# Chunked attention with a token-selecting feed-forward layer: V laid over 60 consecutive partitions, loaded on two queues

## The chip, the cores and the metric

One NeuronCore of a Trainium2 chip runs the whole program. The metric is device time in microseconds, from the first to the last instruction with what lies around them; lower is better. The program has five instruction streams (TensorE or PE, VectorE or DVE, ScalarE or ACT, GpSimd or POOL, SyncE or SP). DMAs are issued from SP and ACT (hardware queues) and from POOL (the software queue, the only one here whose DMAs cast from float32 to float16 on the way), and sixteen DMA engines carry them all out.

## The reference

Four batches, eight heads, 768 tokens of 64 numbers. The tokens are cut in chunks of 32. A chunk attends to eight memory keys and to the tokens from 16 before it to 8 after it:

```python
for c in range(nc):                      # 24 chunks of 32 tokens
    l_start, r_end = max(0, c_start - 16), min(S, c_end + 8)
    k_full = concat([mem_k, k[:, :, l_start:r_end]]); v_full = concat([mem_v, v[:, :, l_start:r_end]])
    scores = matmul(q_c, k_full.T) / sqrt(D)
    a = exp(scores - max); a = a / sum(a)
    out[:, :, c_start:c_end] = matmul(a, v_full)
# x = out with the heads side by side: (4, 768, 512); then per batch:
s = x @ w_gate; top = the 128 tokens with the largest s
ye = relu(x[top] @ w1) @ w2              # 512 -> 1024 -> 512
out[top] = x[top] + sigmoid(s[top]) * ye
```

## The kernel before

**Tiling.** Work goes by pairs of heads (head i and head i+4 of a batch): 16 pairs n = 0 to 15, four to a batch. Three chunks form a group of 96 queries, eight groups to a pair. The context of a group is 120 tokens in a row (16 before, 96, 8 after). Of them the 60 even-odd token pairs and four rows of memory make the 64 rows of one head; two heads fill the 128 partitions. A V row holds two tokens (128 float32, 512 B). `t[partition, pair and group, 128]` in `vbufs` holds one batch; there are two such buffers.

**The layout before.** Row 16 jj + t of a head's 64 partitions holds the token pair 4t + jj, and rows 15, 31, 47 and 63 hold memory. So one head's V takes four DMAs of 15 partitions (L96), and `mem_v` goes to four partitions, one DMA for each pair (L103). K is transposed on PE into `p_t` and copied by DVE into `kw` in the same order of columns (L225); POOL adds the memory columns (L232).

**Order.** `tc.manual_schedule()` keeps each engine's instructions in the order in which the code issues them, and an engine waits at the first of its instructions that isn't ready. The loop over n issues: scores of pair n+1 (PE matmuls L258, ACT exponentials L263), `tr_k` of n+2, values of n (PE, L284), `cast_v` of n+2 (ACT L240 for six groups, DVE L242 for the first and last), second half of the scores, `tr_q` of n+3, second half of the values, `normalise` (DVE L291, L292). The steps of the feed-forward layer of the batch before are spread over the four pairs of a batch by `moe_steps`. One of them is `m_x16` (L336): the cast of x to float16, in three DVE instructions for a batch.

**Loads.** The q and k of a batch go through POOL (L80, cast to float16), V through SP (a part of the first pair through ACT). Batch 0 is loaded at the start, batch 1 and the weights (`load_w`, L198, L199) after the prologue, batch b+2 after the third pair of batch b. A DMA gets one of eight completion semaphores for the hardware queues (another eight for the software queue), and waits until the earlier DMA with the same one has landed.

Of the kernel before, what the change touches and what calls it, by code (L numbers as in the profile page):

```python
# [26 lines left out]
def kernel(  # L27
# [13 lines left out]
    nc = tc.nc  # L41
# [40 lines left out]

    def load_v(b, p0, n, engines=(nc.sync, nc.sync)):


        t = vbufs[b % 2].rearrange("p n g d -> p (n g) d")
        for hh in range(2):
            eng = engines[hh]
            h = 4 * hh + p0
            lo = 1 if (b, h) == (0, 0) else 0  # L90
            hi = NG * n - 1 if (b, h + n) == (B - 1, H) else NG * n
            for jj in range(4):
                o = 64 * hh + 16 * jj
                base = (b * H + h) * HD + (2 * jj - 16) * D
                u = NG * p0
                eng.dma_start(out=t[o:o + 15, u + lo:u + hi, :],  # L96
                              in_=_dap(v, base + 96 * D * lo, [[8 * D, 15], [96 * D, hi - lo], [1, 128]]))
                if lo:
                    eng.dma_start(out=t[o + 2:o + 15, u, :], in_=_dap(v, base + 16 * D, [[8 * D, 13], [1, 128]]))
                if hi < NG * n:  # L100
                    eng.dma_start(out=t[o:o + 14, u + hi, :], in_=_dap(v, base + 96 * D * hi, [[8 * D, 14], [1, 128]]))
            for i in range(n):
                eng.dma_start(out=t[64 * hh + 15:64 * hh + 64:16, NG * (p0 + i):NG * (p0 + i + 1), :],  # L103
                              in_=_dap(mem_v, (b * H + h + i) * n_mem * D, [[2 * D, 4], [0, NG], [1, 128]]))


    alloc_batch(0)
    load_qk(0, q, q16s[0], 0, 2, 4)
    load_qk(0, k, k16s[0], 0, 2, 4)
    ident16 = cst.tile([128, 128], F16, tag="ident16")  # L110
# [6 lines left out]
    nc.gpsimd.dma_start(out=memk16, in_=_dap(mem_k, 0, [[D, n_mem], [n_mem * D, B * H], [1, D]]))  # L117
    for h0 in (1, 5):
        load_qk(0, q, q16s[0], h0, 3)
        load_qk(0, k, k16s[0], h0, 3)  # L120

# [4 lines left out]
    for pr, g in ((0, 0), (NP - 1, NG - 1)):  # L126
        nc.vector.memset(vbufs[0 if pr == 0 else 1][:, pr, g, :], 0.0)
    load_v(0, 0, 1, (nc.sync, nc.scalar))
    load_v(0, 1, 3)
    wgb = cst.tile([128, Dm], FP, tag="wgb")  # L130
    nc.sync.dma_start(out=wgb, in_=_dap(moe_w_gate, 0, [[0, 128], [1, Dm]]))

    pi = cst.tile([128, 1], I32, tag="pi")
    nc.vector.tensor_scalar(out=pi, in0=prow, scalar1=15, scalar2=None, op0=ALU.bitwise_and)
    pp = cst.tile([128, 1], FP, tag="pp")
    nc.vector.tensor_copy(out=pp, in_=pi)
    ismem = cst.tile([128, 1], FP, tag="ismem")
# [446 lines left out]
```

## Time and profile before

| | us |
|---|---|
| median of three runs | 194.24 (193.93 to 195.65) |
| the profiled execution, its own time | 193.39 |
| span from first to last instruction in it | 191.7 |
| PE busy | 116.6 (61%) |
| DVE busy | 89.0 (46%) |
| ACT busy | 72.4 (38%) |
| POOL busy | 31.1 (16%) |
| DMA share of the chain that ended last | 37% |

The profile is of one execution. Busy time is that of the whole span; the chain that ended last is followed back from the last instruction, at each step to what released it. GB/s count the bytes as they land, so a load that casts float32 to float16 counts half of what it reads.

### The profile page before, as it was taken

The numbers are of one execution on the slowest core, as the hardware profiler recorded it, in microseconds if no ns is written. First come the engines' busy times: TensorE is split into PE (matmuls) and PEld (weight loads), VectorE is DVE, ScalarE is ACT, GpSimd is POOL, SyncE is SP. The second block draws the span as 40 slices with busy tenths as digits, with TensorE's granted clock in tenths as the row PEclk, the third lists the DMA queues.
The fourth block names the chain that finished last, engine by engine and source line by source line (L and its number), as shares of the span: only waits on it lengthen the run. The fifth ranks groups of instructions, "written<-read, shape, count | busy, mean of one in ns | idle before, by whom it ended". The sixth has DMA issues, their size and how long they took to land.

```text
span 191.7 us, 5338 instructions
## 1 busy us (share of the span) xinstructions
PE 116.6 (61%) x2280; PEld 95.5 (50%) x2280; DVE 89.0 (46%) x285; ACT 72.4 (38%) x152; POOL 31.1 (16%) x55
## 2 busy tenths in 40 slices
PE   0052750799000006999998977799988676745840
PEld 0041640688000005878887656698657565423810
DVE  2222001451000014699943799942799693478010
ACT  0040801961000017776447588148595031110210
POOL 7400910106000000000230220001220000030030
PEclk9999999999999999999999999559995557885596
DMA  5999999999999697999999993900048200047304
GB/s 75 207 203 113 120 166 221 187 208 204 214 208 186 83 107 69 119 90 263 214 135 180 207 177 89 270 9 3 3 56 258 77 0 0 3 56 224 107 0 55
DMA packets 29681, 24.76 MB, mean 129 GB/s; under 512 B 1892, under 2 KB 25432, under 8 KB 29656
## 3 DMA queue, kind: packets, MB, share of 16 engines
q1 hardware_dynamic: 19976, 14.68, 43.4%
q0 software_dynamic: 9104, 9.47, 32.9%
q8 instruction: 18, 0.29, 0.7%
q10 hardware_dynamic: 576, 0.26, 0.6%
q14 instruction: 7, 0.06, 0.1%
HBM read 25.49 MB, written 7.34 MB: 171 GB/s over the span
## 4 chain that ended last, share of the span: by engine, by line
DMA 37%; DVE 25%; PE 22%; issue 6%; SPq 5%; ACT 1%; POOLq 1%; ACTq 0%; DVEq 0%
DMA v<-in_v_dram 25%; DMA v<-in_mem_v_dram 7%; DVE junk L329 6%; PE p_x L284 6%; DVE gr L366 5%; SPq L96 4%; PE p_m L428 4%; DMA out_dram<-x 3%; DVE x L292 3%; PE p_m L437 3%; PE p_t L208 3%; PE p_m L403 3%; DVE x L336 3%; DMA out_dram<-y,idx 3%; PE p_s L258 3%
## 5 line engine op out<-in xcount | busy, mean ns | idle before, releaser
L263 ACT ACTIVATE es<-p_s,maskb 128x256 f16<-128x256 f32 x96 | 38.5, 477 | 24.6 <-PE p_s L258 24.6
L284 PE MATMUL p_x<-vc,es 64*96 64x65 f16 (+1 forms) x768 | 32.0, 235 | 1.3 <-DVE x L292 0.7
L208 PE MATMUL p_t<-ident,k 96*64 96x96 f16 x256 | 11.9, 253 | 31.3 <-ACT qT L216 28.4
L284 PEld LDWEIGHTS <-es 64*96 64x96 f16 (+1 forms) x768 | 25.5, 136 | 6.2 <-issue 1.7
L242 DVE TENSOR_SCALAR vc<-v,ones 128x128 f16<-128x128 f32 x32 | 8.8, 343 | 39.8 <-DMA v<-in_v_dram 26.2
L240 ACT CAST vc<-v 128x768 f16<-128x768 f32 x16 | 13.5, 845 | 35.6 <-DMA v<-in_v_dram 26.9
L232 POOL COPY kw<-memkT 128x64 f16<-128x64 f16 x16 | 9.1, 566 | 104.1 <-DVE kw L225 67.3
L208 PEld LDWEIGHTS <-k 96*64 96x64 f16 x256 | 9.5, 141 | 32.9 <-issue 27.4
L258 PE MATMUL p_s<-qT,kw 64*64 64x96 f16 x512 | 23.4, 253 | 0.5 <-ACT es L263 0.5
L258 PEld LDWEIGHTS <-kw 64*64 64x64 f16 x512 | 18.3, 141 | 4.3 <-issue 2.0
L208 PE MATMUL p_t<-ident,q 96*64 96x96 f16 x256 | 12.5, 258 | 10.4 <-DVE kw L225 9.8
L225 DVE COPY kw<-p_t 128x512 f16<-128x512 f16 x32 | 12.1, 419 | 11.4 <-PE p_t L208 10.5
L208 PEld LDWEIGHTS <-q 96*64 96x64 f16 x256 | 10.3, 145 | 12.1 <-issue 10.6
L329 DVE SCALAR_TENSOR_TENSOR junk<-x,wgb 128x512 f32<-128x512 f32 (+2 forms) x30 | 16.0, 580 | 0.1
L292 DVE TENSOR_TENSOR x<-p_x,rd 128x768 f32<-128x768 f32 x16 | 15.3, 958 | 0.6
L216 ACT COPY qT<-p_t 128x768 f16<-128x768 f16 x16 | 13.0, 810 | 6.3 <-PE p_t L208 6.2
L441 POOL DMA_INDIRECT out_dram<-y,idx x4 | 6.8, 1701 | 49.8 <-DVE y L440 27.8
L366 DVE TENSOR_SCALAR gr<-brow,scr 128x768 f16<-128x768 f32 x24 | 13.3, 614 | 0.1
L291 DVE RECIPROCAL rd<-p_x 128x12 f32<-128x12 f32 x16 | 3.7, 229 | 18.6 <-PE p_x L284 18.6
L403 PEld LDWEIGHTS <-x 128*128 128x128 f16 x96 | 9.8, 143 | 1.3 <-DVE sel L395 0.7
L428 PEld LDWEIGHTS <-w_sb 128*128 128x128 f16 x128 | 8.8, 110 | 3.2 <-DVE gate L418 2.4
L376 PEld LDWEIGHTS <-gr 128*128 128x128 f16 x144 | 5.4, 105 | 8.2 <-DVE gr L366 7.8
(89 smaller groups left out, 112.0 us busy)
## 6 DMA issues: line engine op xcount, KB each, us to landing
v<-in_v_dram SPq DMA_DIRECT2D x20, 240.0 KB
out_dram<-x SPq DMA_DIRECT2D x4, 1152.0 KB
q<-in_q_dram POOLq DMA_DIRECT2D x6, 384.0 KB, 12.8
k<-in_k_dram POOLq DMA_DIRECT2D x6, 384.0 KB, 13.4
w_sb<-in_moe_w_dram POOLq DMA_DIRECT2D x2, 1024.0 KB, 22.3
out_dram<-x SPq DMA_DIRECT2D x4, 384.0 KB
v<-in_v_dram SPq DMA_DIRECT2D x8, 180.0 KB
v<-in_v_dram SPq DMA_DIRECT2D x4, 232.5 KB
```

Source lines behind the costliest of these rows:

```text
L208: nc.tensor.transpose(out=p_t[64 * h:64 * h + 64, j, 2:98], in_=src[b][:, pr + 4 * h, 64 * j:64 * j + 64], identity=ident16[0:96, 0:96])
L216: nc.scalar.copy(out=qT, in_=p_t[:, :, 2:98].rearrange("p j t -> p t j"))
L225: nc.vector.tensor_copy(out=kw[:, :, s, :].rearrange("p g (j t) -> p g j t", t=16), in_=_sap(p_t, 100 * s, [[12, NG], [200, 4], [1, 16]]))
L240: nc.scalar.copy(out=vc[:, 1:7, :, 0:64], in_=vt[:, pr, 1:7, :].rearrange("p g (s d) -> p g s d", d=D))
L258: nc.tensor.matmul(out=p_s[o:o + 64, s, 96 * gi:96 * gi + 96], lhsT=kw[o:o + 64, g, s, :], rhs=qf[o:o + 64, 96 * g:96 * g + 96], start=Tru ...
L263: nc.scalar.activation(out=es[:, :, :, 32 * c:32 * c + 32], in_=pv[:, :, :, 32 * c:32 * c + 32], func=AF.Exp, bias=maskb[:, c:c + 1], scal ...
L284: nc.tensor.matmul(out=p_x[r0:r1, h, c0:c0 + 65], lhsT=es[o:o + 64, s, gi, q0:q1], rhs=vc[o:o + 64, GROUPS[half][gi], s, :], start=(s == 0 ...
L292: nc.vector.tensor_tensor(out=xs[b].rearrange("p g (h n d) -> p n h g d", n=NP, d=D)[:, pr], in0=pv[:, :, :, 0:64], in1=rd.to_broadcast([1 ...
L329: nc.vector.scalar_tensor_tensor(out=o, in0=i, scalar=1.0, in1=w, op0=ALU.mult, op1=ALU.mult, accum_out=dst[:, bl:bl + 1])
L366: nc.vector.tensor_scalar(out=m.gr[:, bl, :], in0=m.brow, scalar1=m.scr[:, bl:bl + 1], scalar2=None, op0=ALU.is_lt)
L403: nc.tensor.matmul(out=p_e[:, 0, 128 * dch:128 * dch + 128], lhsT=m.x16[:, bl, 128 * dch:128 * dch + 128], rhs=m.sel[:, bl, :], start=(bl ...
L428: nc.tensor.matmul(out=p_h[:, 0, 128 * fi:128 * fi + 128], lhsT=w1_sb[:, dch, f0:f0 + 128], rhs=m.xeT[:, dch, :], start=(dch == 0), stop=( ...
```

## The change

V: a head's 60 token pairs go to 60 consecutive partitions in token order (o = 0 for the first head of a pair, 64 for the second), memory to the last four. The four 15-partition DMAs of a head become one of 60 partitions; the first head's goes on SP, the second's on ACT. All `mem_v` loads go on SP, behind the V loads. The columns of `kw`, the masks and `ones8` follow the same order. K is loaded ahead of q at the start, and batch 0 is loaded pair by pair. `m_x16` runs on ACT instead of DVE. Line numbers of the changed kernel are two to three higher from about L94 on (the cast of V is L243, the copy of K L228, `m_x16` L339).

```diff
-    def load_v(b, p0, n, engines=(nc.sync, nc.sync)):
+    def load_v(b, p0, n, engines=(nc.sync, nc.scalar)):
         t = vbufs[b % 2].rearrange("p n g d -> p (n g) d")
+        u = NG * p0
         for hh in range(2):
...
-            for jj in range(4):
-                o = 64 * hh + 16 * jj
-                base = (b * H + h) * HD + (2 * jj - 16) * D
-                u = NG * p0
-                eng.dma_start(out=t[o:o + 15, u + lo:u + hi, :],
-                              in_=_dap(v, base + 96 * D * lo, [[8 * D, 15], [96 * D, hi - lo], [1, 128]]))
...
+            o = 64 * hh
+            base = (b * H + h) * HD - 16 * D
+            engines[hh].dma_start(out=t[o:o + 60, u + lo:u + hi, :],
+                                  in_=_dap(v, base + 96 * D * lo, [[2 * D, 60], [96 * D, hi - lo], [1, 128]]))
...
+        for hh in range(2):
             for i in range(n):
-                eng.dma_start(out=t[64 * hh + 15:64 * hh + 64:16, NG * (p0 + i):NG * (p0 + i + 1), :],
-                              in_=_dap(mem_v, (b * H + h + i) * n_mem * D, [[2 * D, 4], [0, NG], [1, 128]]))
+                nc.sync.dma_start(out=t[64 * hh + 60:64 * hh + 64, u + NG * i:u + NG * (i + 1), :],
+                                  in_=_dap(mem_v, (b * H + 4 * hh + p0 + i) * n_mem * D,
+                                           [[2 * D, 4], [0, NG], [1, 128]]))
...
+    load_qk(0, k, k16s[0], 0, 2, 4)
     load_qk(0, q, q16s[0], 0, 2, 4)
-    load_qk(0, k, k16s[0], 0, 2, 4)
...
-    for h0 in (1, 5):
-        load_qk(0, q, q16s[0], h0, 3)
-        load_qk(0, k, k16s[0], h0, 3)
+    for pr in range(1, NP):
+        load_qk(0, k, k16s[0], pr, 2, 4)
+        load_qk(0, q, q16s[0], pr, 2, 4)
...
-    load_v(0, 0, 1, (nc.sync, nc.scalar))
-    load_v(0, 1, 3)
+    load_v(0, 0, 1)
+    load_v(0, 1, 1)
+    load_v(0, 2, 2)
...
         for s in range(2):
-            nc.vector.tensor_copy(out=kw[:, :, s, :].rearrange("p g (j t) -> p g j t", t=16),
-                                  in_=_sap(p_t, 100 * s, [[12, NG], [200, 4], [1, 16]]))
+            nc.vector.tensor_copy(out=kw[:, :, s, 0:60].rearrange("p g (t j) -> p g t j", j=4),
+                                  in_=_sap(p_t, 100 * s, [[12, NG], [1, 15], [200, 4]]))
...
-        nc.gpsimd.tensor_copy(out=kw.rearrange("p g s (j t) -> p g (s j) t", t=16)[:, :, :, 15],
-                              in_=memkT[:, n:n + 1, :, :].rearrange("p o s j -> p o (s j)").to_broadcast([128, NG, 8]))
+        nc.gpsimd.tensor_copy(out=kw[:, :, :, 60:64],
+                              in_=memkT[:, n, :, :].unsqueeze(1).to_broadcast([128, NG, 2, 4]))
...
-        nc.vector.tensor_copy(out=o, in_=i)
+        nc.scalar.copy(out=o, in_=i)
```

**SP, from the last load of batch 0 to the refill of its buffer.** `v_0` and `v_1` are the two V buffers (`v_1` takes batch 1). Before:

```order
L131 DMA wgb<-in_moe_w_gate_dram 128x512
L96 DMA v_1_85<-in_v_dram 15x32x128 x4
L103 DMA v_1_85<-in_mem_v_dram 4x8x128 x4
L96 DMA v_1_85<-in_v_dram 15x32x128 x4
L103 DMA v_1_85<-in_mem_v_dram 4x8x128 x4
L96 DMA v_0_84<-in_v_dram 15x32x128 x4
```

Now, from the top of the queue:

```order
L94 DMA v_0_84<-in_v_dram 60x16x128
L103 DMA v_0_84<-in_mem_v_dram 4x8x128 x4
L133 DMA wgb<-in_moe_w_gate_dram 128x512
L94 DMA v_1_85<-in_v_dram 60x32x128
L103 DMA v_1_85<-in_mem_v_dram 4x8x128 x8
L94 DMA v_0_84<-in_v_dram 60x32x128
```

Eight V DMAs of batch 1 have become one, and all eight memory loads follow it; the other half has left this queue.

**ACT, from the cast of pair 1 to that of pair 2**, as it stands now, with the semaphores waited for (DMAHW: a DMA of a hardware queue):

```order
L219 COPY qT<-p_t 128x768 [waits PE_49]
L243 CAST vc_150<-v_0_84 128x12x64 [waits DMAHW4_49,DMAHW7_49,DMAHW1_49,DMAHW0_49]
L94 DMA v_1_85<-in_v_dram 60x32x128 [waits DMAHW2_49]
L266 ACTIVATE es<-p_s,maskb 128x8x32 [waits PE_49]
L266 ACTIVATE es<-p_s,maskb 128x8x32 x2
L243 CAST vc_153<-v_0_84 128x12x64 [waits DMAHW6_49,DMAHW5_49,DMAHW3_49]
```

The second half of batch 1's V is issued here, behind the cast of pair 1; before, no DMA stood between these casts.

**POOL, from the memory columns of pairs 0 and 1 to batch 1's loads** (DMASW: a DMA of the software queue). Before:

```order
L80 DMA k_0_87<-in_k_dram 96x3x512
L232 COPY kw_158<-memkT 128x64 [waits DVE_49]
L232 COPY kw_161<-memkT 128x64 [waits DVE_49]
L80 DMA q_1_354<-in_q_dram 96x4x512
L80 DMA k_1_355<-in_k_dram 96x4x512 [waits DMASW0_49]
```

Now:

```order
L80 DMA q_0_86<-in_q_dram 96x2x512 [waits DMASW0_49]
L235 COPY kw_148<-memkT 128x16x4 [waits DVE_49]
L235 COPY kw_151<-memkT 128x16x4
L80 DMA q_1_344<-in_q_dram 96x4x512 [waits DMASW1_49]
L80 DMA k_1_345<-in_k_dram 96x4x512 [waits DMASW2_49]
```

The copy for pair 1 no longer waits for DVE, and batch 1's q and k stand right behind it.

## Rows read from the trace of the kernel before

**Rows 1.** The page: busy time by engine, and 40 slices of the span.

```profile
PE 116.6 (61%) x2280; PEld 95.5 (50%) x2280; DVE 89.0 (46%) x285; ACT 72.4 (38%) x152; POOL 31.1 (16%) x55
...
DMA  5999999999999697999999993900048200047304
```

**Rows 2.** Chain that ended last, 0 to 75: start, us, what.

```profile
32.34 22.39 DMA v<-in_v_dram
...
57.96 12.92 DMA v<-in_mem_v_dram
```

**Rows 3.** Timeline of ACT: start, us, engine, line, names, shapes, count [idle before].

```profile
32.90 0.83 ACT L240 CAST vc<-v 128x768 f16<-128x768 f32 x1 [8.71 <-DMA v<-in_mem_v_dram]
...
42.81 1.20 ACT L263 ACTIVATE es<-p_s,maskb 128x256 f16<-128x256 f32 x3 [0.73 <-PE p_s L258]
70.95 0.84 ACT L240 CAST vc<-v 128x768 f16<-128x768 f32 x1 [26.94 <-DMA v<-in_v_dram]
```

**Rows 4.** Timeline of SP's queue, the issues of batch 1's V.

```profile
25.01 12.06 SPq L96 DMA_DIRECT2D v<-in_v_dram  x4
...
57.96 4.30 SPq L103 DMA_DIRECT2D v<-in_mem_v_dram  x4
```

**Rows 5.** Timeline of POOL, pair 1's memory columns and batch 1's first load.

```profile
18.89 0.45 POOL L232 COPY kw<-memkT 128x64 f16<-128x64 f16 x1 [6.62 <-DVE kw L225]
19.06 0.72 POOL L80 DMA_DIRECT2D q<-in_q_dram  x1
```

**Rows 6.** Busy time by stretch; the last two columns are DMA share and GB/s landed.

```profile
0.00:5.00 5.00, 0.00 (x0) 0.00 (x0) 1.61 (x16) 0.00 (x0) 3.74 (x12) 1.00 0.54 81
...
15.00:20.00 5.00, 1.97 (x41) 1.67 (x43) 1.35 (x4) 0.24 (x1) 1.11 (x3) 1.00 1.19 108
...
33.00:47.00 14.00, 12.29 (x264) 10.57 (x263) 6.11 (x20) 9.28 (x20) 2.99 (x6) 1.00 1.17 200
47.00:61.00 14.00, 0.94 (x23) 0.78 (x18) 0.00 (x0) 0.00 (x0) 1.17 (x2) 1.00 1.17 210
61.00:71.00 10.00, 0.00 (x0) 0.00 (x0) 0.03 (x1) 0.05 (x1) 0.00 (x0) 1.00 0.81 100
```

**Rows 7.** DMA issues of the whole run: names, queue, count, KB each (1,024 B).

```profile
v<-in_v_dram SPq DMA_DIRECT2D x20, 240.0 KB
...
q<-in_q_dram POOLq DMA_DIRECT2D x6, 384.0 KB, 12.8
...
w_sb<-in_moe_w_dram POOLq DMA_DIRECT2D x2, 1024.0 KB, 22.3
...
v<-in_mem_v_dram SPq DMA_DIRECT2D x31, 16.0 KB
wgb<-in_moe_w_gate_dram SPq DMA_DIRECT2D x1, 256.0 KB
```

**Rows 8.** DMA traffic from 143.9 to 150.5 us, the store of batch 2's x.

```profile
DMA packets 801, 1.59 MB, mean 241 GB/s; under 512 B 32, under 2 KB 32, under 8 KB 800
```

**Rows 9.** Instruction groups by shape: count, busy us, mean ns of one, idle before.

```profile
L292 DVE TENSOR_TENSOR x<-p_x,rd 128x768 f32<-128x768 f32 x16 | 15.3, 958 | 0.6
...
L240 ACT CAST vc<-v 128x768 f16<-128x768 f32 x16 | 13.5, 845 | 35.6 <-DMA v<-in_v_dram 26.9 <-DMA v<-in_mem_v_dram 8.7
...
L225 DVE COPY kw<-p_t 128x512 f16<-128x512 f16 x32 | 12.1, 419 | 11.4 <-PE p_t L208 10.5 <-ACT es L263 0.9
...
L336 DVE CAST x<-x 128x1024 f16<-128x1024 f32 x9 | 5.9, 686 | 0.0
```

**Rows 10.** Chain that ended last, in batch 1's first pairs.

```profile
85.47 1.20 DVE x L336 x2
```

**Rows 11.** Busy time by stretch, columns PE, PEld, DVE, ACT, POOL, in pair 5.

```profile
85.00:91.00 6.00, 6.00 (x120) 4.76 (x116) 5.81 (x16) 4.26 (x11) 0.46 (x1) 1.00 0.83 219
```

**Rows 12.** Timeline of DVE, the last two casts of x and what follows the first.

```profile
158.50 1.35 DVE L336 CAST x<-x 128x2304 f16<-128x2304 f32 x1
159.77 0.15 DVE L416 TENSOR_SCALAR idx<-p_m 128x1 int32<-128x1 f32 x1
...
174.38 0.55 DVE L336 CAST x<-x 128x768 f16<-128x768 f32 x1
```

More of the change, by code (lines that the diff above doesn't have):

```diff
@@ L81, in load_qk @@
                             in_=_dap(src, (b * H + h0) * HD, [[512, 96], [step * HD, n], [1, 512]]))
-    def load_v(b, p0, n, engines=(nc.sync, nc.sync)):
+    def load_v(b, p0, n, engines=(nc.sync, nc.scalar)):
         t = vbufs[b % 2].rearrange("p n g d -> p (n g) d")
+        u = NG * p0
         for hh in range(2):
-            eng = engines[hh]
             h = 4 * hh + p0
@@ L91, in load_v @@
             hi = NG * n - 1 if (b, h + n) == (B - 1, H) else NG * n
-            for jj in range(4):
-                o = 64 * hh + 16 * jj
-                base = (b * H + h) * HD + (2 * jj - 16) * D
-                u = NG * p0
-                eng.dma_start(out=t[o:o + 15, u + lo:u + hi, :],
-                              in_=_dap(v, base + 96 * D * lo, [[8 * D, 15], [96 * D, hi - lo], [1, 128]]))
[L98 to L101, printed above, removed]
+            o = 64 * hh
+            base = (b * H + h) * HD - 16 * D
+            engines[hh].dma_start(out=t[o:o + 60, u + lo:u + hi, :],
+                                  in_=_dap(v, base + 96 * D * lo, [[2 * D, 60], [96 * D, hi - lo], [1, 128]]))
+            if lo:
+                engines[hh].dma_start(out=t[o + 8:o + 60, u, :], in_=_dap(v, base + 16 * D, [[2 * D, 52], [1, 128]]))
+            if hi < NG * n:
+                engines[hh].dma_start(out=t[o:o + 56, u + hi, :],
+                                      in_=_dap(v, base + 96 * D * hi, [[2 * D, 56], [1, 128]]))
+        for hh in range(2):
             for i in range(n):
-                eng.dma_start(out=t[64 * hh + 15:64 * hh + 64:16, NG * (p0 + i):NG * (p0 + i + 1), :],
-                              in_=_dap(mem_v, (b * H + h + i) * n_mem * D, [[2 * D, 4], [0, NG], [1, 128]]))
+                nc.sync.dma_start(out=t[64 * hh + 60:64 * hh + 64, u + NG * i:u + NG * (i + 1), :],
+                                  in_=_dap(mem_v, (b * H + 4 * hh + p0 + i) * n_mem * D,
+                                           [[2 * D, 4], [0, NG], [1, 128]]))
     alloc_batch(0)
+    load_qk(0, k, k16s[0], 0, 2, 4)
     load_qk(0, q, q16s[0], 0, 2, 4)
-    load_qk(0, k, k16s[0], 0, 2, 4)
     ident16 = cst.tile([128, 128], F16, tag="ident16")
@@ L133 @@
     pi = cst.tile([128, 1], I32, tag="pi")
-    nc.vector.tensor_scalar(out=pi, in0=prow, scalar1=15, scalar2=None, op0=ALU.bitwise_and)
-    pp = cst.tile([128, 1], FP, tag="pp")
-    nc.vector.tensor_copy(out=pp, in_=pi)
+    nc.vector.tensor_scalar(out=pi, in0=prow, scalar1=63, scalar2=None, op0=ALU.bitwise_and)
+    kp = cst.tile([128, 1], FP, tag="kp")
+    nc.vector.tensor_copy(out=kp, in_=pi)
     ismem = cst.tile([128, 1], FP, tag="ismem")
-    nc.vector.tensor_scalar(out=ismem, in0=pp, scalar1=14.5, scalar2=None, op0=ALU.is_gt)
+    nc.vector.tensor_scalar(out=ismem, in0=kp, scalar1=59.5, scalar2=None, op0=ALU.is_gt)
     maskb = cst.tile([128, 3], FP, tag="maskb")
@@ L141 @@
     for c in range(3):
-        nc.vector.tensor_scalar(out=maskb[:, c:c + 1], in0=pp, scalar1=4.0 * c - 0.5, scalar2=None, op0=ALU.is_gt)
-        nc.vector.tensor_scalar(out=tmpm[:, c:c + 1], in0=pp, scalar1=4.0 * c + 6.5, scalar2=None, op0=ALU.is_lt)
+        nc.vector.tensor_scalar(out=maskb[:, c:c + 1], in0=kp, scalar1=16.0 * c - 0.5, scalar2=None, op0=ALU.is_gt)
+        nc.vector.tensor_scalar(out=tmpm[:, c:c + 1], in0=kp, scalar1=16.0 * c + 27.5, scalar2=None, op0=ALU.is_lt)
     nc.vector.tensor_tensor(out=maskb, in0=maskb, in1=tmpm, op=ALU.mult)
@@ L150 @@
     nc.vector.memset(ones8, 1.0)
-    nc.vector.tensor_scalar(out=ones8[:, 0:1], in0=pp, scalar1=1.5, scalar2=None, op0=ALU.is_gt)
-    nc.vector.tensor_scalar(out=ones8[:, 7:8], in0=pp, scalar1=14.0, scalar2=None, op0=ALU.not_equal)
+    nc.vector.tensor_scalar(out=ones8[:, 0:1], in0=kp, scalar1=7.5, scalar2=None, op0=ALU.is_gt)
+    nc.vector.tensor_scalar(out=ones8[:, 7:8], in0=kp, scalar1=55.5, scalar2=None, op0=ALU.is_lt)
+    nc.vector.tensor_tensor(out=ones8[:, 7:8], in0=ones8[:, 7:8], in1=ismem, op=ALU.max)
     vcs, kws = [], []
```

## The prediction, made before the changed kernel ran

> **What bounds the kernel now.** I read the page first: no engine is busy for more than 61% of the span, while the row of the DMA engines shows nines from the second slice to the 26th and little behind that [rows 1]. So the first two thirds are a matter of loads. The chain of waits says which: from 32 to 71 us its long pieces are landings of V and of the memory rows of V [rows 2]. The timeline of ACT shows where the engines stand still for them. There are two stalls. The first, 8.7 us, ends at 32.9, when the memory rows for pair 1 are there. The second, 26.9 us, ends at 70.95, when batch 1's V is there for the cast of pair 4 [rows 3]. ACT had been through with everything else at 42.81 + 1.20 = 44.0. From 70.95 on the program runs without a long wait for a load, and 191.7 - 70.95 = 120.75 us of the span follow. The question is therefore when the cast of pair 4 can start.
>
> Why V is late: SP issues batch 1's V from 25.0 to 62.3 [rows 4], in turn with POOL's q, k and weights. While both queues work, 200 to 210 GB/s land. While V is alone it is 100 to 108 GB/s, though the engines count as busy [rows 6]; a store of x, whose DMAs span 96 and 32 partitions, reaches 241 GB/s [rows 8]. The V loads, 15 partitions at a time, are slow by themselves. POOL also loses time: it waited 6.6 us for DVE before pair 1's memory columns, and batch 1's first q stood behind them, until 19.06 [rows 5].
>
> **The change part by part.**
>
> *V over 60 partitions, two queues.* What has to land before pair 4's cast: V of two batches (2 x 8 x 240 KB = 3.93 MB), their memory rows (2 x 8 x 16 KB = 0.26), the gate row (0.26), q and k of batches 0 and 1 (2 x 4 x 384 KB = 3.15; batch 0 is as many bytes in other pieces), and, ahead of it or beside it, the weights (2.10) [rows 7]: 9.70 MB. Batch 2's q and k (1.57) may come before or behind; with them it is 11.27 MB. In the first 5 us, 81 GB/s x 5 = 0.41 MB land. The rest at 205 GB/s, between the two rows with both queues at work [rows 6], takes (9.70 - 0.41) / 0.205 = 45.3 us, or 53.0 with batch 2's part: the cast starts at 50.3 or 58.0. The premise is that the stretches at 100 GB/s vanish, because the 60-partition halves land as freely as the store. I take 55, in the upper half, because SP's queue now holds all memory rows behind its half of V, and pair 4 needs the fifth of the eight. Gain: 70.95 - 55 = 15.95 us.
>
> The Trainium skill, page "SBUF — State Buffer", section "Door 1: The DMA port swizzle", says that 16 partitions in a row reach four of sixteen ports, at 104 GB/s measured for 1 MiB, and 64 reach eight, at 196. The trace agrees for the first: 108 GB/s. No row shows the second. By the page V alone would double its rate, which supports the premise and leaves the sum as it is.
>
> *POOL's copies no longer wait for DVE; k ahead of q; batch 0 by pairs.* They bring batch 1's q forward by up to the 6.6 us [rows 5], which is part of the uninterrupted rate above, and make pairs 0 and 1 ready sooner. Both lie ahead of the cast of pair 4, so I add nothing for them. That cover is gone only if V comes as early as pair 4 asks (first rival).
>
> *ACT issues a half of V.* The issue stands behind the cast of pair 1, so batch 1's second half can't start before that. It is one instruction, and the exponentials behind it would wait for the same loads anyway: nothing.
>
> *The copy of K on DVE.* 512 elements took 419 ns, reading 16 in a row [rows 9]. Now 480 are read with a step of 200 elements. At worst an element costs what the float32 product from PSUM costs, 958 / 768 = 1.25 ns: 599 ns, 0.18 more; at best nothing changes. I take 0.18, as the read is no longer in a row. In batches 1 to 3 DVE sets the pace in two of four pairs (5.81 busy of 6.00 in one [rows 11]); there it counts: 2 copies x 2 pairs x 3 batches x 0.18 = +2.2 us. The ends are 0 and, with all 22 copies from pair 5 on, +4.0.
>
> The Trainium skill, page "VectorE: DVE Perf Modes", section "Mode 2×_1P — pack two bf16 into one 32-bit read", wants a step of one between 16-bit elements for two results a cycle, which speaks against this part of the change. The 419 ns bear it out for the old order; by the rule the new order loses the pairing, and the sum stays.
>
> *The cast of x, from DVE to ACT.* On DVE three casts a batch, of which two stand in the chain: 1.20 us [rows 10], for three batches -3.6. The last batch's large cast stood for 159.77 - 158.50 = 1.27 us ahead of the index that the feed-forward layer waits for [rows 12]: -1.3. Its small one (0.55 [rows 12]) is ahead of the last mask: -0.5, or nothing if something else is late there. On ACT a cast of 1,024 columns costs 845 / 768 x 1024 = 1.13 us by V's cast [rows 9]. Two of three fall in pair 5, where ACT was busy for 4.26 of 6.00 us [rows 11]: 6.5 us of work in 6.0, so +0.5 us for each of three batches, +1.5. The ends are 0 (it runs into the next pair's room) and 9 x 1.13 = +10, which would need ACT on the path throughout; 3 is a fair end. Sum of DVE and ACT: 2.2 - 3.6 - 1.3 - 0.5 + 1.5 = -1.7, from -5.4 to +3.
>
> *The rest* (masks, one more operation on DVE at the start, the shape of POOL's copy) lies in time in which these engines waited for loads: nothing.
>
> **Sum.** 193.39 (the profiled execution's own time) - 15.95 - 1.7 = 175.7. The median of the runs is 0.85 above the profiled execution, so 176.6; I say **176**. With the cast at 50.3 or 58.0 and the ends of the DVE and ACT terms it is 168 to 183.
>
> **Rivals.**
>
> *A. V is served first.* Two hardware queues against one software queue may take two turns in three. Then V, q and k of two batches would land ahead of the weights: 4.46 + 3.15 = 7.61 MB, at 5 + 7.2 / 0.205 = 40 us. Pair 4 asks at 44.0 - 8.7 = 35.3 at the earliest, so 40 decides. Gain 30.9 instead of 15.95: 162. For it: the second hardware queue. Against it: one queue of V was slow beside POOL's, 25 to 71 us for 2.1 MB [rows 3, 4].
>
> *B. V is no faster.* The limit could lie in the 512-byte rows and not in the partitions, and then 60 at a time and two queues change nothing; only POOL's 6.6 us come back. The cast starts at 64.4: 193.39 - 6.6 - 1.7 + 0.85 = 186. For it: packets and bytes are the same. Against it: beside POOL's wide loads the same engines land twice as much [rows 6]. The Trainium skill, page "DMA: Bandwidth & Descriptors", section "Rules for kernel authors", says of two transfers to disjoint partition halves that they serialise, and that spreading DMAs over issuing engines brings no bandwidth. By that rule the second queue is worth nothing; the trace does not contradict it, since no row has two full halves at once.
>
> *C. Slower: the 60-partition DMA runs on few of the sixteen engines.* All DMAs of V would then sit on, say, four. An engine's share of 210 GB/s is 13 GB/s, four give 52, and 4.46 MB take 85 us: the cast starts at 87, 16 us later than now, 193.39 + 16 - 1.7 + 0.85 = 209. It turns slower where the cast starts after 70.95 + 1.7 = 72.7, that is under 4.46 MB / 71 us = 63 GB/s for V, fewer than five engines. Against it: the 15-partition DMAs moved 108 GB/s [rows 6], over eight engines' share, and 60 is a multiple of 15.
>
> **Chances.** My forecast 0.65, A 0.13, B 0.15, C 0.07. The likeliest, 176, is the prediction. 160 to 188 holds A, the forecast with its ends and B; C and an even earlier or later V stay out, some 0.15. This kernel's measurement tells about 1% (2 us) from no change. Faster by over 1%: the forecast, A and 0.10 of B, 0.88. Within 1%: 0.04 of B, where the copy of K and ACT eat the 6.6 us, and 0.01 of C: 0.05. Slower: the rest, 0.07.
>
> **What would show it.** The cast of V ahead of pair 4 starts at 50 to 58 and is still the longest wait of ACT. No stretch before it lands less than 150 GB/s after the first 5 us. POOL issues batch 1's q by 13 us. The copy of K takes near 0.6 us, the cast of x about 1.13 on ACT; the time from pair 4's cast to the end is 118 to 121 us. A wait on ACT of more than 0.5 us a batch behind a cast of x, a cast of pair 4 before 45 or after 62, or a longer tail after it would each show a term wrong.

## The result, and the profile after

The changed kernel takes **177.9 us** (median of 4 runs, 176.82 to 179.89). The kernel before took 194.94 beside it on the same chip (193.93 to 196.33): the ratio is 0.910, interval 0.901 to 0.919. Some executions of a kernel take a few per cent longer than its others; the medians here are of all runs, the ratios leave those out. The forecast was 176. The profiled execution took 178.1 us, its span is 176.3; that of before was 193.39 with a span of 191.7, so the span became 15.4 us shorter. The forecast had 15.95 + 1.7 = 17.65.

The page of the changed kernel answers [rows 1]. Engines first, then the 40 slices; the last row is the mean GB/s.

```profile
PE 118.3 (67%) x2280; PEld 95.9 (54%) x2280; DVE 88.5 (50%) x275; ACT 82.8 (47%) x163; POOL 28.5 (16%) x57
...
DMA  5999999999999898999920465000159000059104
GB/s 127 215 223 205 229 216 226 231 227 218 209 194 269 217 116 156 290 264 181 189 60 5 63 200 161 6 0 4 13 128 279 10 0 4 0 77 294 51 0 59
```

The nines now end with the 20th slice, not the 26th, and the GB/s under them stay above 200 from the second slice to the eleventh. The same stretches as in [rows 6] (the last two columns are DMA share and GB/s):

```profile
0.00:5.00 5.00, 0.00 (x0) 0.00 (x0) 1.62 (x16) 0.00 (x0) 3.74 (x12) 1.00 0.60 132
...
15.00:20.00 5.00, 2.36 (x48) 1.95 (x47) 1.46 (x3) 2.08 (x2) 4.48 (x14) 1.00 1.14 214
...
33.00:47.00 14.00, 9.57 (x208) 8.15 (x207) 4.05 (x8) 4.22 (x10) 2.64 (x6) 1.00 1.16 221
47.00:61.00 14.00, 8.93 (x192) 7.63 (x193) 7.48 (x19) 9.18 (x20) 0.24 (x1) 1.00 1.08 231
```

15 to 20 us went from 108 to 214 GB/s: the stretches in which V was alone and slow are gone. From 55 to 61 us, when batch 2's V is nearly alone, 260 GB/s land. The timeline of ACT shows what that did to the stalls of [rows 3], and a new one:

```profile
37.43 1.21 ACT L266 ACTIVATE es<-p_s,maskb 128x256 f16<-128x256 f32 x3 [0.73 <-PE p_s L261]
49.39 0.83 ACT L243 CAST vc<-v 128x768 f16<-128x768 f32 x1 [10.75 <-DMA v<-in_mem_v_dram]
49.69 0.33 ACTq L94 DMA_DIRECT2D v<-in_v_dram  x1
...
79.37 0.33 ACTq L94 DMA_DIRECT2D v<-in_v_dram  x1
79.74 5.86 ACTq L99 DMA_DIRECT2D v<-in_v_dram  x1
85.64 1.20 ACT L266 ACTIVATE es<-p_s,maskb 128x256 f16<-128x256 f32 x3 [5.75 <-issue]
```

Read it in three steps. The stall ahead of pair 1 is gone. The cast of pair 4 starts at 49.39, not 70.95: **21.56 us earlier**, where 15.95 were forecast, after a wait of 10.75 and not 26.94. But from there to the end of the span it is 176.3 - 49.39 = 126.9 us, against 120.75 before: **6.2 us of the gain are given back**. The lower three rows show where. ACT issues two V DMAs of batch 3 in a row, and the second one, 56 rows of 512 B (28 KB), occupies ACT's queue for 5.86 us; the exponentials behind it wait 5.75 us for "issue", that is for nothing that the profile can name. On DVE, the division that closes a pair shows the cost:

```profile
76.64 0.23 DVE L294 RECIPROCAL rd<-p_x 128x12 f32<-128x12 f32 x1 [0.44 <-PE p_x L287]
91.13 0.23 DVE L294 RECIPROCAL rd<-p_x 128x12 f32<-128x12 f32 x1 [8.61 <-PE p_x L287]
```

This pair takes 14.49 us. Two groups of instructions answer [rows 9], the copy of K and the cast of x (mean ns of one behind the comma):

```profile
L228 DVE COPY kw<-p_t 128x480 f16<-128x480 f16 x32 | 19.5, 650 | 13.7 <-PE p_t L211 13.7
...
L339 ACT CAST x<-x 128x1024 f16<-128x1024 f32 x9 | 9.7, 1077 | 0.0
```

POOL did not do as forecast either. The row that answers [rows 5] (issue of batch 1's first q) stands at 15.65, where the forecast said by 13 (it was 19.06):

```profile
15.30 0.41 POOL L235 COPY kw<-memkT 128x64 f16<-128x64 f16 x2 [7.20 <-DVE memkT L172]
15.65 0.70 POOL L80 DMA_DIRECT2D q<-in_q_dram  x1
```

POOL no longer waits for the copy of K, but 7.20 us for the memory keys: PE waits for their DMA until 13.89, where it was 9.15 before.

### The profile page after: what moved, and what is told of

Same layout as the page of the kernel before. It is cut to its first block, busy times and chain, and to the rows that moved or that the text cites. A ratio compares the mean times of both kernels' runs of the same rounds, so it can differ in the third digit from the quotient of the medians.

```text
span 176.3 us, 5308 instructions
## 1 busy us (share of the span) xinstructions
PE 118.3 (67%) x2280; PEld 95.9 (54%) x2280; DVE 88.5 (50%) x275; ACT 82.8 (47%) x163; POOL 28.5 (16%) x57
## 4 chain that ended last, share of the span: by engine, by line
DMA 31%; PE 28%; DVE 18%; ACT 7%; issue 7%; ACTq 4%; POOLq 1%; SPq 0%; DVEq 0%
DMA v<-in_v_dram 19%; PE p_x L287 8%; DMA v<-in_mem_v_dram 6%; DVE gr L369 6%; PE p_t L211 5%; DVE junk L332 5%; PE p_m L440 4%; DMA out_dram<-x 4%; PE p_s L261 4%; PE p_m L431 3%; ACTq L99 3%; PE p_m L406 3%; ACT es L266 3%; DMA out_dram<-y,idx 3%; DVE x L295 2%
## 5 line engine op out<-in xcount | busy, mean ns | idle before, releaser
L266 ACT ACTIVATE es<-p_s,maskb 128x256 f16<-128x256 f32 x96 | 38.9, 489 | 26.1 <-PE p_s L261 20.4
L228 DVE COPY kw<-p_t 128x480 f16<-128x480 f16 x32 | 19.5, 650 | 13.7 <-PE p_t L211 13.7
L243 ACT CAST vc<-v 128x768 f16<-128x768 f32 x16 | 13.8, 861 | 10.8 <-DMA v<-in_mem_v_dram 10.8
L211 PEld LDWEIGHTS <-q 96*64 96x64 f16 x256 | 10.1, 149 | 5.3 <-issue 4.2
L245 DVE TENSOR_SCALAR vc<-v,ones 128x128 f16<-128x128 f32 x32 | 7.6, 290 | 10.4 <-DMA v<-in_mem_v_dram 10.0
L339 ACT CAST x<-x 128x1024 f16<-128x1024 f32 (+2 forms) x11 | 12.6, 1148 | 0.0
L431 PE MATMUL p_m<-xeT,w_sb 128*128 128x128 f16 x96 | 7.2, 236 | 5.5 <-ACT hT L433 4.5
```

Source lines behind the costliest of these rows:

```text
L211: nc.tensor.transpose(out=p_t[64 * h:64 * h + 64, j, 2:98], in_=src[b][:, pr + 4 * h, 64 * j:64 * j + 64], identity=ident16[0:96, 0:96])
L228: nc.vector.tensor_copy(out=kw[:, :, s, 0:60].rearrange("p g (t j) -> p g t j", j=4), in_=_sap(p_t, 100 * s, [[12, NG], [1, 15], [200, 4]]))
L243: nc.scalar.copy(out=vc[:, 1:7, :, 0:64], in_=vt[:, pr, 1:7, :].rearrange("p g (s d) -> p g s d", d=D))
L266: nc.scalar.activation(out=es[:, :, :, 32 * c:32 * c + 32], in_=pv[:, :, :, 32 * c:32 * c + 32], func=AF.Exp, bias=maskb[:, c:c + 1], scal ...
L339: nc.scalar.copy(out=o, in_=i)
L431: nc.tensor.matmul(out=p_h[:, 0, 128 * fi:128 * fi + 128], lhsT=w1_sb[:, dch, f0:f0 + 128], rhs=m.xeT[:, dch, :], start=(dch == 0), stop=( ...
```

## The experiments

All kernels ran beside the kernel before (194.7 to 194.9 us); ratios are to it.

| kernel | us | ratio, interval |
|---|---|---|
| the change | 177.9 | 0.910, 0.901 to 0.919 |
| one queue for V | 183.16 | 0.940, 0.931 to 0.948 |
| one queue, 15 partitions at a time | 204.62 | 1.051, 1.043 to 1.060 |
| before, with early q and k | 194.54 | 0.984, 0.974 to 0.994 |
| small DMA on SP | 172.96 | 0.888, 0.881 to 0.895 |
| small DMA first, on ACT | 173.16 | 0.880, 0.871 to 0.888 |
| cast of x on DVE | 181.13 | 0.931, 0.926 to 0.937 |
| copy of K done twice | 188.26 | 0.964, 0.955 to 0.974 |
| small on SP, K read in a row | 179.77 | 0.933, 0.920 to 0.945 |
| small and memory rows first | 175.68 | 0.910, 0.899 to 0.920 |
| small on SP, weights late | **169.67** | 0.877, 0.862 to 0.891 |
| the same, V earlier | 173.50 | 0.891, 0.884 to 0.898 |

### V loads alone

Only batch 2's V is loaded, six times in six forms, each waited for by one small copy on DVE; all else of the computation is left out.

```python
    rows = t[o + 16 * jj:o + 16 * jj + 15] if form == "15row" else t[o + jj:o + 60:4]
...
for form, engs in (("15row", (SP, SP)), ("15step", (SP, SP)), ("60", (SP, SP)), ("60", (SP, ACT)),
                   ("15row", (SP, ACT)), ("15step", (SP, ACT))):
```

> Only V loads of one batch (1.97 MB), six times one after the other with nothing beside them; the rest of the program is left out. Order: four DMAs of 15 neighbouring partitions per half on SP; four DMAs of 15 partitions in steps of four per half on SP; one of 60 per half on SP; one of 60 per half, SP and ACT; then the first two forms with the halves on SP and ACT. If the reach of partitions is the limit (theory P): about 19 us (105 GB/s) for the first, 8 to 11 us (180 to 240 GB/s) for the second and third, 7 to 10 us for the fourth, and the fifth between 10 and 19 us. If the number of queues is what counts (theory Q): the first three alike, and the last three alike and faster. If the number of DMAs counts: the second as slow as the first, the third fast.

It ran once. The timeline of DVE; what stands in brackets is the wait for 1.97 MB of V:

```profile
25.46 0.19 DVE L72 COPY col<-vt 128x32 f32<-128x32 f32 x1 [20.34 <-DMA vt<-in_v_dram]
39.54 0.19 DVE L72 COPY col<-vt 128x32 f32<-128x32 f32 x1 [13.88 <-DMA vt<-in_v_dram]
52.25 0.20 DVE L72 COPY col<-vt 128x32 f32<-128x32 f32 x1 [12.52 <-DMA vt<-in_v_dram]
63.30 0.19 DVE L72 COPY col<-vt 128x32 f32<-128x32 f32 x1 [10.85 <-DMA vt<-in_v_dram]
81.06 0.19 DVE L72 COPY col<-vt 128x32 f32<-128x32 f32 x1 [17.56 <-DMA vt<-in_v_dram]
93.06 0.19 DVE L72 COPY col<-vt 128x32 f32<-128x32 f32 x1 [11.82 <-DMA vt<-in_v_dram]
```

On SP alone: four DMAs of 15 neighbouring partitions a half take 20.34 us (97 GB/s), four of 15 partitions with a step of 4 take 13.88, one of 60 takes 12.52 (157 GB/s). The second and the first have the same number of DMAs, rows and bytes; only the reach over partitions differs, and it makes 6.5 of the 7.8 us. A second queue takes 12.52 to 10.85, 13% less time, and the 15 neighbouring partitions from 20.34 to 17.56. The order is that of theory P; the second to fourth forms are slower than it had them (8 to 11 and 7 to 10 us).

The mean GB/s in 40 slices, first of the load with 60 partitions on one queue (39.9 to 52.2), then on two (52.6 to 63.2):

```profile
GB/s 0 0 30 147 230 301 226 203 223 191 148 143 143 160 186 160 158 170 190 188 182 190 223 206 203 206 196 195 195 190 195 195 195 186 193 163 75 7 0 0
```

```profile
GB/s 0 0 0 56 189 234 294 274 187 180 168 147 147 182 269 294 288 292 288 294 288 292 288 294 288 292 288 284 294 228 170 151 155 158 120 50 0 0 0 0
```

With two queues some 290 GB/s land through fourteen slices in a row; with one queue it is 143 to 230 in all slices but one between the first and the last few.

The Trainium skill, page "SBUF — State Buffer", section "Can I just issue two DMAs to hit both halves?", says that two DMAs at once, one at partition 0 and one at 64, gained 6% over a single one and that they serialise. Here the second queue gives 12.52 / 10.85 = 1.15 times the rate over the whole wait, and some 290 GB/s while both halves are under way, which the halves one after the other do not hold; the measurement decides, though over the whole wait the direction (much less than twice) agrees.

### One queue for V

```diff
-    def load_v(b, p0, n, engines=(nc.sync, nc.scalar)):
+    def load_v(b, p0, n, engines=(nc.sync, nc.sync)):
```

> The changed kernel with both halves of V on SP. Theory P: V still lands freely, so the cast of pair 4 starts at 50 to 56 us (49.4 with two queues), and as ACT then issues no DMA its stop of 5.9 us at 79.7 goes away; time 172 to 180. Theory Q: with one turn in two beside POOL's loads V is back where it was, the cast starts at 62 to 68, time 184 to 190.

183.16 us, 5.3 more than the change, although ACT now issues no V; with the 4.9 us that its hold costs the change (below) the second queue is worth up to 10.2. The time lies between the two expectations, and so does the cast of pair 4 at 59.84, some 10 us later than with two queues. The profiled execution is one of the two longest (189.0), so this row is a rough place only.

```profile
59.84 0.83 ACT L243 CAST vc<-v 128x768 f16<-128x768 f32 x1 [19.46 <-DMA v<-in_mem_v_dram]
```

So the second queue is worth more beside POOL's loads (some 10 us at the cast, for two batches of V) than alone (1.67 us for one batch). The Trainium skill, page "DMA: Bandwidth & Descriptors", section "Queues, rings and completion order", says that each DMA engine goes round between the queues that have work for it. By that, V with two of three queues gets more turns than with one of two; the two runs agree, but no run here separates this from a lesser hold on SP's own queue.

### One queue, 15 partitions at a time

The same with each half in four pieces, rows still in token order:

```diff
+            for jj in range(4):
+                engines[hh].dma_start(out=t[o + 15 * jj:o + 15 * jj + 15, u + lo:u + hi, :], ...
```

> As e1, both halves on SP and the same layout, but each half in four DMAs of 15 neighbouring partitions. Theory P: the stretches at about 100 GB/s come back and the cast of pair 4 starts 6 us or more later than in e1, 58 to 68; time 6 to 14 us over e1. Theory Q or POOL's earlier loads as the cause: within 3 us of e1.

204.62, so 21.5 us over the kernel with 60 at a time and more than before. Time and cast are both beyond either expectation. The stretches show the old sign again, 105 GB/s at a DMA share of 0.61 and 1.19:

```profile
70.73 0.83 ACT L245 CAST vc<-v 128x768 f16<-128x768 f32 x1 [19.51 <-DMA v<-in_v_dram]
...
61.00:71.00 10.00, 0.00 (x0) 0.00 (x0) 0.23 (x2) 0.27 (x1) 0.00 (x0) 1.00 0.61 105
71.00:85.00 14.00, 11.60 (x229) 9.69 (x229) 9.89 (x28) 10.63 (x23) 0.91 (x2) 1.00 1.19 105
...
90.48 0.61 PE L213 MATMUL p_t<-ident,k 96*64 96x96 f16 x10 [4.49 <-issue]
123.20 1.13 PE L289 MATMUL p_x<-vc,es 64*96 64x65 f16 x23 [4.99 <-issue]
```

At 70.73 the cast of pair 4 is back where it was before the change (70.95). So without the reach and the second queue, all other parts of the change together do not move this cast. The reach brings it to 59.84 and the second queue to 49.39: 10.9 and 10.5 us, about equal, as far as the one long execution with one queue goes.

The 21.5 us of the whole time are more than these 10.9. Behind the cast PE stands still for 4.49, 1.45 and 4.99 us, in the middle of a group of matmuls and for nothing that the profile names; with one queue and 60 partitions it is 2.01 and 2.98, and the kernel before has no such stop of 1 us. What causes them is not shown, so the whole time does not say what the reach is worth.

### Before, with q and k early

```diff
+    alloc_batch(1)
+    for h0 in (0, 4):
+        load_qk(1, q, q16s[1], h0, 4)
+        load_qk(1, k, k16s[1], h0, 4)
     mem_keys()
```

> The kernel before, with nothing changed but that batch 1's q and k are issued ahead of everything that POOL waits for in the prologue (in the changed kernel POOL has no such wait of 6.6 us). Theory of the prediction, rival B: this part alone brings batch 1's q forward by 6.6 us and at most that much comes off, 188 to 191. Rival: V's own 15-partition DMAs set the end and nothing comes back, 193 to 196; the first memory rows may even land later (V shares the engines with q earlier), up to 198.

The median is 194.54 (10 runs, 189.94 to 197.52), beside 194.86 for the kernel before. The ratio of 0.984 rests on the two shortest of the ten alone; by the medians no gain can be told from none. The profile says why: batch 1's q is issued at 7.00, 12 us earlier, and the stall is only moved.

```profile
43.54 0.83 ACT L240 CAST vc<-v 128x768 f16<-128x768 f32 x1 [19.48 <-DMA v<-in_mem_v_dram]
...
69.90 0.83 ACT L240 CAST vc<-v 128x768 f16<-128x768 f32 x1 [15.24 <-DMA v<-in_mem_v_dram]
```

Pair 1's wait grew from 8.71 to 19.48 us and pair 4's cast starts at 69.90, not 70.95. POOL's order alone brings 1 us at the cast of pair 4, and new waits for memory rows stand ahead of pairs 8 and 12 (4.15 and 1.10 us).

### The hold on ACT: small DMA on SP, and small DMA first

```diff
-                engines[hh].dma_start(out=t[o:o + 56, u + hi, :],
+                nc.sync.dma_start(out=t[o:o + 56, u + hi, :],
```

> The changed kernel with the one small DMA of the last group of batch 3 (56 partitions, 28 KB) issued on SP instead of ACT behind the large one. If ACT stands still there because a second DMA on its queue can't be issued until the large one ahead has been taken up (theory H): the stop of 5.9 us and the slower pair behind it (1.9 us) go, time 169 to 172.5. If other work would have been late there anyway: less than 2 us gained.

172.96 us. ACT issues one DMA in 0.33 us and goes on; SP's queue is occupied instead, where nothing waits (first ACT, then SP; how much of SP's 11.74 us is the same hold is not shown):

```profile
80.70 0.33 ACTq L94 DMA_DIRECT2D v<-in_v_dram  x1
81.37 1.20 ACT L266 ACTIVATE es<-p_s,maskb 128x256 f16<-128x256 f32 x3
```

```profile
69.93 11.74 SPq L99 DMA_DIRECT2D v<-in_v_dram  x1
```

The second form leaves both on ACT and only changes places: the issue of the 56 rows (then L95) stands ahead of the large one (L97).

> The changed kernel, in which the one place where ACT issues two DMAs of V in a row (batch 3, a small one of 28 KB behind one of 930 KB) has them in the other order, small one first, both still on ACT. Theory: an issue is held while a large DMA ahead of it on the same queue is being taken up; then the large one behind the small one is not held, ACT goes on within 1 us, and the time is that of the kernel that has the small one on SP (172.96), 172.5 to 174. Rival: two DMAs in a row on ACT hold it whatever their order (a queue that holds one): the hold of some 5 us stays, 177 to 179.

173.16 us, and no hold:

```profile
78.48 0.34 ACTq L95 DMA_DIRECT2D v<-in_v_dram  x1
78.91 0.35 ACTq L97 DMA_DIRECT2D v<-in_v_dram  x1
79.31 1.20 ACT L266 ACTIVATE es<-p_s,maskb 128x256 f16<-128x256 f32 x3 [0.25 <-ACT xeT L410]
```

So it is not two issues in a row that hold, but an issue behind a large one (31 x 60 rows of 512 B) on the same queue. The kernel with the cast of x on DVE, which has the order of the change, shows the hold again (4.96 us). By the medians the change pays 4.7 to 4.9 us for the order of two lines.

### Cast of x on DVE

```diff
-        nc.scalar.copy(out=o, in_=i)
+        nc.vector.tensor_copy(out=o, in_=i)
```

> The changed kernel with the cast of x back on DVE (m_x16, eleven instructions). Theory of the prediction: the change won 3.6 + 1.3 + 0.5 on DVE and paid 1.5 on ACT with this part, so putting it back costs 3.9 us: 177.9 + 3.9 = 181.8, the last pair of heads 2.0 to 2.6 us longer (10.55 us between its divisions before, 7.93 with the cast on ACT). Rival: DVE waits elsewhere in the middle batches and only the last batch counts (1.3 + 0.5 = 1.8, and 1.5 comes back on ACT): 178 to 180. A gain below 177 would say that ACT is the engine that the change overloads.

181.13: 3.2 us over the change, near the 3.9 of the prediction, and over the 178 to 180 of the rival. But the place is not the prediction's. The division of pair 2, first in the change, then here:

```profile
49.83 0.22 DVE L294 RECIPROCAL rd<-p_x 128x12 f32<-128x12 f32 x1
```

```profile
50.58 0.23 DVE L294 RECIPROCAL rd<-p_x 128x12 f32<-128x12 f32 x1
```

The last pair, from its predecessor's division to its own: in the change, here, and with the small DMA on SP (the third number from the right is the granted clock):

```profile
142.25:150.18 7.93, 6.25 (x110) 5.61 (x109) 4.28 (x18) 3.79 (x4) 0.00 (x0) 0.82 0.01 2
```

```profile
142.24:152.79 10.55, 7.55 (x110) 6.79 (x109) 5.55 (x19) 1.78 (x3) 0.00 (x0) 0.73 0.01 2
```

```profile
136.50:145.63 9.13, 7.45 (x110) 6.64 (x109) 4.29 (x17) 3.79 (x4) 0.00 (x0) 0.69 0.01 2
```

All casts of the first three batches lie between the divisions of pairs 2 and 14. That stretch takes 142.25 - 49.83 = 92.4 us in the change and 142.24 - 50.58 = 91.7 here: with the cast on DVE it is no longer. The last pair takes 10.55 and not 7.93, 2.6 us more. With the small DMA on SP and the cast on ACT it takes 9.13 at a clock of 0.69, so up to 1.2 of the 2.6 us may be the clock's and not the cast's (1 stands for 2.4 GHz, 0.5 for 1.2; these are means of both levels).

### Copy of K done twice

```diff
+            for _ in range(2):
                 nc.vector.tensor_copy(out=kw[:, :, s, 0:60]. ...
```

> The changed kernel with each copy of K out of PSUM done twice, 32 more copies of 0.65 us on DVE; 22 of them lie behind the cast of pair 4 in the program's order. Theory of the prediction: a microsecond of the copy counts in two of four pairs, 12 of 22 copies: +12 x 0.65 = 7.8 us, 185.7; by that slope the 0.23 us that a copy has grown cost 2.8 us. Rival 1: DVE has room, +2 us or less. Rival 2: each copy is on the path, since PE's transposes of q wait for the PSUM buffer that the copy empties: 22 x 0.65 = 14 us, 192.

188.26, 10.4 us more:

```profile
L229 DVE COPY kw<-p_t 128x480 f16<-128x480 f16 x64 | 40.5, 654 | 15.9 <-PE p_t L211 14.7
```

DVE works 40.5 - 19.5 = 21.0 us more, so a microsecond of the copy costs 0.50 us, between the prediction's way of counting (7.8) and rival 2 (14).

### K read in a row

```diff
-            nc.vector.tensor_copy(out=kw[:, :, s, 0:60].rearrange("p g (t j) -> p g t j", j=4),
-                                  in_=_sap(p_t, 100 * s, [[12, NG], [1, 15], [200, 4]]))
+            nc.vector.tensor_copy(out=kw[:, :, s, 0:60].rearrange("p g (t j) -> p g j t", j=4),
+                                  in_=_sap(p_t, 100 * s, [[12, NG], [200, 4], [1, 15]]))
```

> The changed kernel with the small DMA of batch 3's V on SP (172.96), and the copy of K walked in the other order: PSUM is read 15 elements in a row and kw written with a step of 4 elements, where the change reads with a step of 200 and writes in a row. Theory of the prediction (the step of the read costs the 0.23 us that a copy has grown): the copy falls to about 0.42 us, and by the slope of the doubled copies (10.4 us for 32 more of 0.65 us, 0.5 us for 1) 32 x 0.23 x 0.5 = 3.7 us come off: 169 to 170. Rival: a step on either side costs the same, the copy stays at 0.6 to 0.65 us and the time at 172 to 174.

179.77, 6.8 us over its base of 172.96, outside both expectations:

```profile
L228 DVE COPY kw<-p_t 128x480 f16<-128x480 f16 x32 | 38.7, 1313 | 14.3 <-PE p_t L211 14.3
```

The step that moved from the read to the write costs twice as much: 1,313 ns for 480 elements against 650. The change's choice, to read with a step and write in a row, is the cheaper of the two; 419 ns had both in rows. Here 38.7 - 19.5 = 19.2 us of DVE cost 6.8, 0.35 us for one (8.7 and 0.45 by the ratios, which take out the difference between chips). I first had the faster copy in mind and was wrong.

### Small ones first, memory rows too

```diff
+        if b > 0:
+            mem_rows()          # the eight mem_v DMAs of the batch, ahead of V
         for hh in range(2):
```

> The changed kernel with small ones first: the 28 KB DMA of batch 3 ahead of the large one on ACT (173.16), and for batches 1 to 3 the eight memory-row DMAs ahead of SP's half of V, not behind it. Theory: the cast of pair 4 waits for memory rows that SP could not issue while its large V DMA was being taken up; with them first, it waits for V alone, which has landed by 41 on SP and 46 on ACT (the same queues' landings in the run with the small DMA on SP): cast at 46 to 47.5 and 170.5 to 172. Rival: bytes set it, the memory rows land with the last of them anyway, and the cast stays at 48.5 to 51, 172.5 to 174.

175.68, 2.5 us over the kernel with the small DMA first alone. Pair 4 now waits for V, and longer:

```profile
53.65 0.83 ACT L248 CAST vc<-v 128x768 f16<-128x768 f32 x1 [15.41 <-DMA v<-in_v_dram]
```

SP's queue tells why: the eight memory DMAs take 9 us, and V is issued at 27.75, where it was 17.68 (first this kernel, then the one with the small DMA first alone).

```profile
17.64 9.03 SPq L91 DMA_DIRECT2D v<-in_mem_v_dram  x8
27.75 0.32 SPq L105 DMA_DIRECT2D v<-in_v_dram  x1
```

```profile
17.68 0.38 SPq L97 DMA_DIRECT2D v<-in_v_dram  x1
```

Both of my expectations failed: I had priced eight small DMAs at nothing. That the profile names the memory rows as the last to land does not mean that they should go first.

### Weights late, and V earlier

```diff
-    load_w()                    # ahead of the loop over pairs
...
+            if b == 0:
+                load_w()        # behind the loads of batch 2, after pair 2
```

> The changed kernel with the small DMA of batch 3's V on SP (172.96), and the weights (2.10 MB as they land) loaded behind batch 2's V, not ahead of batch 1's landing. Theory of the prediction's sum, bytes over a rate of 205 to 230 GB/s: 9 us less has to land ahead of pair 4, its cast goes from 50.7 to 41.5 and the time to 164 (165 if part of it comes back in a later wait). Rival 1: V's own queues set the landing, the cast moves by 2 us or less, 171 to 173. Rival 2: the weights are then late for the first feed-forward step of pair 4 or 5 and the gain turns into a wait of PE there, 170 to 176.

169.67, the shortest median, 3.3 us under its base, though the intervals of the two ratios overlap (0.862 to 0.891, 0.881 to 0.895). It is outside all three expectations. Pair 4's cast moved by 5.5 us (50.72 to 45.19), not by 9, and a new wait stands ahead of pair 8:

```profile
45.19 0.83 ACT L243 CAST vc<-v 128x768 f16<-128x768 f32 x1 [7.55 <-DMA v<-in_mem_v_dram]
...
72.03 0.83 ACT L243 CAST vc<-v 128x768 f16<-128x768 f32 x1 [4.79 <-DMA v<-in_mem_v_dram]
```

The weights are issued at 34.16, still ahead of pair 4's cast, so only part of their bytes left the way. A part of the gain is given back a batch later, in the wait ahead of pair 8. That batch 2's V then shares the DMA engines with the weights is the likely reason; no run shows it.

The last run issues V earlier too: `load_v(1, 0, NP)` behind batch 0's V, and batch b+2's V ahead of the cast that waits.

> The kernel with the small DMA on SP and the weights late (169.67), and V issued earlier: batch 1's V right behind batch 0's (ACT's half was issued at 23.68, behind the cast of pair 1), batches 2 and 3 ahead of the cast that waits (ACT's half of batch 2 was issued at 45.50, behind the cast of pair 4, and pair 8 then waited 4.79 us for batch 2's memory rows). Theory: what is left of the waits is the time of issue on ACT; pair 8's wait falls to 1 us or less, pair 4's cast (45.19) moves to 42 to 44.5, and the time is 164.5 to 167. Rival 1: bytes set both waits (the DMA row stands at 210 to 240 GB/s until 61), their sum stays and the time is 168.5 to 171. Rival 2: batch 1's V takes the engines from batch 0's q and k, the first division moves from 30 to 33 or later and the start loses what the casts win: 171 to 174.

173.50, 3.8 us worse than without it by the medians (the intervals of the ratios overlap). Both waits grew:

```profile
47.00 0.83 ACT L244 CAST vc<-v 128x768 f16<-128x768 f32 x1 [8.55 <-DMA v<-in_mem_v_dram]
...
75.43 0.83 ACT L244 CAST vc<-v 128x768 f16<-128x768 f32 x1 [6.38 <-DMA v<-in_mem_v_dram]
```

Issue on ACT was not the limit. On SP the memory rows of batch 1 now start at 34.41, where they started at 15.95 (first this kernel, then its base):

```profile
34.41 8.30 SPq L103 DMA_DIRECT2D v<-in_mem_v_dram  x8
```

```profile
15.95 24.10 SPq L103 DMA_DIRECT2D v<-in_mem_v_dram  x8
```

They are through at 42.7, 2.7 us later than before, and pair 4's cast, which waits for them, is 1.8 us later. What held them is not shown. What orders the loads best was not settled.

## Why the prediction was right or wrong

**V's landing: mechanism right, size too small.** The prediction put the cast of pair 4 at 55; it starts at 49.39, just ahead of the earlier bound of 50.3. By the stretches, 10.5 MB had landed by then, between the 9.70 and 11.27 MB of the prediction. Three numbers make the 5.6 us. The first 5 us carried 132 GB/s and not 81, 0.25 MB or 1.2 us. The rest came at (10.5 - 0.66) / 44.4 = 222 GB/s, not 205, which is 3.7 us. And "the upper half, because SP's queue now holds all memory rows" cost 0.8 us that were not there: the chain of waits goes through ACT's half of V, issued at 24.67 and landed at 49.23, and the memory rows land with it. The reasons hold: the loads alone and the kernel with 15 partitions show the reach, the kernel with one queue shows the second queue. Of the other parts only the cast of x was tried by itself, but the kernel with 15 partitions on one queue has all of them, and its cast of pair 4 stands at 70.73.

**"ACT issues a half of V: nothing" is the step that failed.** It looked at batch 1 alone, where the issue stands behind a cast that waits anyway. In batch 3 two issues stand in a row, and the second holds ACT for 5.86 us. The trace of before could have warned: SP's queue shows 12.06 us for four V DMAs [rows 4]. On SP only further DMAs stand behind such an issue; on ACT exponentials do. Two kernels that remove the hold show 4.7 to 4.9 us.

**The copy of K.** 0.18 us more was forecast and called the worst (599 ns); 0.23 was measured (650 against 419 ns). At 0.35 to 0.50 us for a microsecond of copying, 32 x 0.231 = 7.4 us cost 2.6 to 3.7, where the prediction had 2.2, under its end of 4.0. That is an estimate from the slopes of the two kernels with longer copies; no run has the old copy back.

**The cast of x: near by luck.** A cast takes 1.077 us against 1.13, and the net gain is 3.2 against 3.9. But -3.6 + 1.5 of it was to come from the first three batches, and there the run with the cast on DVE shows no gain (92.4 us with the change, 91.7 without). The last pair brought up to 2.6 instead of 1.3, a part of which may be the clock. The end behind it brought 0.5, as forecast (176.3 - 150.18 = 26.1 us against 179.4 - 152.79 = 26.6), and the first three pairs the rest.

**The sum of both** was to be -1.7. The kernel with the small DMA on SP has no hold, and from its cast of pair 4 to its end it is 171.5 - 50.72 = 120.8 us; with the small one first it is 171.4 - 48.98 = 122.4. Against 120.75 before, DVE and ACT come out at 0 to +1.7. In the first of the two PE also stands still for 1.27 us, in the second for 2.80 and 0.98, for nothing that the profile names. Without these stops it would be -1.2 and -2.1, which is an estimate; whether -1.7 was right is open. A slip in the prediction's own ends: the upper one adds up to 4.0 - 3.6 - 1.3 + 3 = +2.1, not +3. Nothing hangs on it.

**So the total is right by two errors of opposite sign.** Forecast: -15.95 - 1.7 = -17.65. Measured: -21.56 at the cast, +6.2 behind it, -15.4.

**Rivals.** A (V first, cast at 40) has its direction only; with the weights late the cast still stands at 45.19. B is out: 60 partitions alone take 12.52 us where 15 take 20.34, and early q and k bring nothing that can be told from none. C is out: the V loads move 157 GB/s alone.

## What to carry to other kernels

Look at how many partitions a DMA reaches before you count its bytes: a stretch in which the engines count as busy at half the GB/s of its neighbours is the sign. Before a DMA issue moves to an engine that also computes, look for the places where two are issued in a row, and put the small one first or on a queue for which no computing waits. That holds for one small DMA: eight of them ahead of V on SP made the kernel 2.5 us slower. And a load that is taken out of the way of one wait must be looked for at the next one.

## What was not expected of the hardware

- An issue behind a large DMA on the same hardware queue held ACT for 5.86 us; with the small one ahead, both issues took 0.34 and 0.35 us.
- For a copy of 480 float16 elements from PSUM, a step of 4 elements on the write (1,313 ns) costs twice as much as a step of 200 on the read (650 ns).
- Eight DMAs of 16 KB ahead of it delayed the issue of a V DMA on SP by 10.1 us (17.68 to 27.75).
- Two halves of V on two queues landed at some 290 GB/s while both were under way, against 143 to 230 for one after the other on one queue.
- PE stopped for 1 to 5 us in the middle of groups of matmuls in some of the other kernels, and neither in the kernel before nor in the change; the profile names no cause.
